# Half of the second output weight on the lower 64 partitions, loaded seven pairs earlier

## The chip, the cores and the metric

The kernel runs on one core of a Trainium2 chip. The metric is the device time of one execution in microseconds, as the median of several runs. Names used below: PE is the matrix engine (PEld its weight load), DVE the vector engine, ACT the scalar engine, POOL the general one, SP the engine that issues nearly all transfers. SBUF is the on-chip memory with 128 partitions, PSUM the accumulator memory of PE, HBM the main memory. Sixteen DMA engines carry the transfers of all queues.

## The reference: what is computed

Two attention blocks, A and B, each for one new token with a cache of 8192 keys and values, 32 heads of 128 elements. Both have one key and value head for each query head, so they are the same computation on different data:

```
q      = (x @ wq)                      # x: 1x512, wq: 512x4096, as 32 heads x 128
scores = q . k_cache * 128**-0.5       # k_cache: 32 x 8192 x 128
p      = softmax(scores)
o      = p @ v_cache                   # v_cache: 32 x 8192 x 128
out    = o (as 1x4096) @ wo            # wo: 4096 x 512
```

The result is the two 512-element rows side by side. All tensors are bf16. The caches are 64 MB each, four of them; wq and wo are 4 MB each. Each byte is used once, so nearly all the work is to move 285 MB from HBM into SBUF.

## The kernel before

The heads are taken in 32 pairs, 16 of A and 16 of B. In a pair, partitions 0 to 63 hold the first head and 64 to 127 the second, and each partition holds 128 consecutive tokens of its head (32 KB). K and V of a pair are one load of 4 MB each, into two buffers each (`kn`, `vn`, selected by the pair's parity).

For a pair `n`:

- `plan_mul` (L244): DVE multiplies K by the broadcast query in four pieces, in place.
- `plan_red` (L250): PE adds up over the 128 elements with the identity as the weight, in two halves of 16 matmuls; `plan_sr` (L263) and `plan_max` (L269) finish the scores and their maximum on DVE.
- `plan_gmax` (L275), `plan_exp` (L285): maximum over the partitions of a head, then the exponential on ACT, with the row sums; `plan_sum` (L304): PE adds the row sums over the partitions, DVE takes the reciprocal.
- `plan_pv` (L311): 128 small matmuls of V with the probabilities, in two halves; `plan_o` (L329) scales the result into two columns of `oD`, which holds for each of the 32 heads a column of 128 elements, one on each partition.

The work of pair n-1 after its exponential is interleaved with the start of pair n. The order on each engine is written out by hand: the main loop (L389 to L435) calls the planning functions, each appends to the engines' programs, and waits are put in where a result of another engine or a load is needed. SP issues every load of K, V and the weights on one queue, in the order of the calls; a K load into a buffer waits until the reduction of two pairs before has read it, a V load until the product of two pairs before has.

The output weight is loaded so that each of the 128 partitions gets consecutive rows (`load_wo`, L199). A group of `n` heads has 128n rows, so partition p holds rows p*n to p*n + n - 1 of the group. Since `oD` has its elements the other way round, `plan_relayout` (L350) turns the columns of a group: DVE spreads them over 128 columns with a mask, one matmul with a selector matrix sums them to the right partitions, and DVE copies the result into `o2`. `plan_wo` (L365) then multiplies: one matmul for each of the `n` rows that a partition holds, with a column of `o2` as the weight and 512 columns of wo, all adding up in one row of `qyp`; `plan_y` (L379) casts that row.

A's wo is one group of 32 heads. It goes into the space of the query weight (`wbuf`), is issued at pair 12, and its 32 matmuls follow in four pieces of eight after pairs 17 to 20. B's wo is split into groups of 16, 8, 4, 2 and 2 heads, so that the relayout of a group can follow as soon as its heads are done (after pairs 23, 27, 29, 30 and 31). All five loads are issued at pair 31, right behind V of pair 31, and all 32 matmuls stand at the end of PE's program, in the order of the groups.

`wo_sb` is a view of `wbuf` as 128 partitions of 32 rows of 512 elements. `jsel` and `mask` are the selector and the mask of a group size, made from the identity at the start (`plan_sel`, L338) for each size in `RG`.

Of the kernel before, what the change touches and what calls it, by code (L numbers as in the profile page):

```python
# [6 lines left out]
ALU = mybir.AluOpType  # L7
AX = mybir.AxisListType
BF16 = mybir.dt.bfloat16
F32 = mybir.dt.float32  # L10

P = 128
# [11 lines left out]
class _Plan:  # L24
# [15 lines left out]
    def op(self, eng, fn, ctr=None, needs=(), inc=1):  # L40

        for m in needs:
            self.wait(eng, m)
        if ctr is None:
            self.prog[eng].append(fn)
            return None
        ctr.n += inc
        self.prog[eng].append(lambda e: fn(e).then_inc(ctr.sem, inc))
        return ctr, ctr.n


def bass_concat_heads__mha_block_cached__gqa_block_cached__decode_kernel(
# [17 lines left out]
    wos = [A_wo, B_wo]  # L70
    NA = 2
    H, Sk, Dh = ks[0].shape[1:]
    D = xs[0].shape[2]
    NOUT = wos[0].shape[1]
# [7 lines left out]
    PA = H // 2  # L82
    NP = NA * PA
# [4 lines left out]
    DW = 512 // HT  # L88
    assert Dh % DW == 0

    WOG = [[(0, 32)], [(0, 16), (16, 8), (24, 4), (28, 2), (30, 2)]]
    RG = [32, 16, 8, 4, 2]

    with ExitStack() as st:
        ec = st.enter_context
# [2 lines left out]
        def sb(name, shape, dt):  # L98
            return ec(nc.sbuf_tensor(name, shape, dt))

        kn = sb("kn", [P, NK, T, Dh], BF16)
        vn = sb("vn", [P, NV, T, Dh], BF16)
        wbuf = sb("wbuf", [P, C * H * Dh], BF16)
        wq_sb = wbuf[:].rearrange("p (c n) -> p c n", c=C)
        wo_sb = wbuf[:].rearrange("p (j n) -> p j n", n=NOUT)
        qbc = sb("qbc", [P, NP, Dh], BF16)
        pt = sb("pt", [P, 2, T, 2], BF16)
        s_sb = sb("s_sb", [P, 2, T], F32)
# [11 lines left out]
        rinv = sb("rinv", [P, NP, 2], F32)  # L120
        oD = sb("oD", [P, NA, H], BF16)
        zb = sb("zb", [P, 2, P], BF16)
        o2 = sb("o2", [P, NA, H], BF16)
        mask = {g: sb("mask%d" % g, [P, P // g], BF16) for g in RG}
        jsel = {g: sb("jsel%d" % g, [P, g], BF16) for g in RG}
        out_sb = sb("out_sb", [1, NA, NOUT], BF16)

        def ps(name, shape):
            return ec(nc.psum_tensor(name, shape, F32))
# [5 lines left out]
        misc = ps("misc", [P, 512])  # L135
        qyp = ps("qyp", [P, 512])

        pl = _Plan()
        op, wait = pl.op, pl.wait

        def ctr(name):
            return _Ctr(nc, st, name)
# [3 lines left out]
        s_wo = [ctr("s_wo%d" % i) for i in range(5)]  # L146
# [4 lines left out]
        c_pool, c_dve, c_act, c_pe = ctr("c_pool"), ctr("c_dve"), ctr("c_act"), ctr("c_pe")  # L151
        c_mul, c_red, c_sr, c_pv = ctr("c_mul"), ctr("c_red"), ctr("c_sr"), ctr("c_pv")

        def dma(eng, dst, src, c, needs=()):
            return op(eng, lambda e: e.dma_start(dst, src), c, needs, inc=16)  # L155
# [21 lines left out]
        k_in, v_in, wq_in, wo_in = {}, {}, {}, {}  # L177
        red_done, pv_done, q_done, wo_done = {}, {}, {}, {}

        def load_k(n):  # L180
            a, i = divmod(n, PA)
            src = ks[a][0, 2 * i:2 * i + 2].rearrange("h (p t) d -> (h p) (t d)", p=HP)
            k_in[n] = dma("SP", kn[:, n % NK].rearrange("p t d -> p (t d)"), src, s_k[n % NK],
                          [red_done.get(n - NK)])

        def load_v(n, parts=1):
            a, i = divmod(n, PA)
            src = vs[a][0, 2 * i:2 * i + 2].rearrange("h (p t) d -> (h p) (t d)", p=HP)
            dst = vn[:, n % NV].rearrange("p t d -> p (t d)")
            w = T * Dh // parts  # L190
            v_in[n] = [dma("SP", dst[:, i * w:(i + 1) * w], src[:, i * w:(i + 1) * w],
                           s_v2 if i else s_v[n % NV], [pv_done.get(n - NV)])
                       for i in range(parts)]

        def load_wq(a):
            wq_in[a] = dma("SP", wbuf[:], wqs[a].rearrange("(p c) n -> p (c n)", p=P), s_w,
                           [q_done.get(a - 1)])

        def load_wo(a, g):  # L199
            h0, n = WOG[a][g]  # L200
            src = wos[a][h0 * Dh:(h0 + n) * Dh, :].rearrange("(p j) n -> p (j n)", p=P)
            wo_in[a, g] = dma("SP", wo_sb[:, h0:h0 + n, :].rearrange("p j n -> p (j n)"), src, s_wo[g],
                              [q_done[NA - 1] if a == 0 else wo_done[0]])


        for a in range(NA):
# [9 lines left out]
        misc_free, qy_free = [x_ready], [x_ready]  # L216
# [25 lines left out]
        mul_done, sr_done, p_done, m_done, r_done, o_done = {}, {}, {}, {}, {}, {}  # L242

        def plan_mul(n, c):  # L244
            k = kn[:, n % NK, c * CT:(c + 1) * CT, :]
            mul_done[n, c] = op("DVE", lambda e: e.tensor_tensor(  # L246
                k, k, qbc[:, n:n + 1, :].broadcast_to([P, CT, Dh]), ALU.mult),
                c_mul, [k_in[n], qbc_ready[n]])
# [87 lines left out]
        sel_ready = {}  # L336

        def plan_sel():  # L338
            for g in RG:
                v = ident[:].rearrange("p (s j) -> p s j", j=g)  # L340
                op("DVE", lambda e, g=g, v=v: e.tensor_reduce(mask[g][:], v, AX.X, ALU.max),
                   c_dve, [i_ident])
                sel_ready[g] = op("DVE", lambda e, g=g, v=v: e.tensor_reduce(
                    jsel[g][:], v.rearrange("p s j -> p j s"), AX.X, ALU.max), c_dve)

        z_n = [0]
        z_free = {}
        o2_ready = {}

        def plan_relayout(a, g):  # L350
            h0, n = WOG[a][g]
            z = z_n[0] % 2
            z_n[0] += 1
            s = P // n
            zv = zb[:, z, :].rearrange("p (h s) -> p h s", s=s)
            m = op("DVE", lambda e: e.tensor_tensor(
                zv, oD[:, a, h0:h0 + n].unsqueeze(2).broadcast_to([P, n, s]),
                mask[n][:, None, :].broadcast_to([P, n, s]), ALU.mult),
                c_dve, [sel_ready[n], o_done[a * PA + (h0 + n) // 2 - 1], z_free.get(z)])
            z_free[z] = op("PE", lambda e: e.matmul(misc[:, 0:n], zb[:, z, :], jsel[n][:],  # L360
                                                    start=True, stop=True), c_pe, [m, misc_free[0]])
            o2_ready[a, g] = misc_free[0] = op("DVE", lambda e: e.tensor_copy(
                o2[:, a, h0:h0 + n], misc[:, 0:n]), c_dve, [z_free[z]])

        def plan_wo(a, g, j0=0, j1=None):  # L365
            h0, n = WOG[a][g]
            j1 = n if j1 is None else j1

            def mm(e):
                r = None  # L370
                for j in range(h0 + j0, h0 + j1):
                    r = e.matmul(qyp[0:1, :], o2[:, a, j:j + 1], wo_sb[:, j, :],  # L372
                                 start=(j == 0), stop=(j == H - 1))
                return r
            wo_done[a] = op("PE", mm, c_pe, [o2_ready[a, g], wo_in[a, g]] + ([qy_free[0]] if h0 + j0 == 0 else []))

        y_done = {}

# [10 lines left out]
        for n in range(NP + 1):  # L389
            last = n == NP  # L390
            if n + 1 < NP:
                load_k(n + 1)
            if not last:
                load_v(n, 2 if n == NP - 1 else 1)
            if n == 0:
                load_wq(1)
            if n == 12:
                load_wo(0, 0)
            if n == NP - 1:
                for g in range(len(WOG[1])):  # L400
                    load_wo(1, g)
            if not last:
                plan_mul(n, 0)
                plan_mul(n, 1)
            if n > 0:
                plan_sum(n - 1)
            if not last:
                plan_red(n, 0)
                plan_mul(n, 2)
                plan_mul(n, 3)  # L410
                plan_sr(n, 0)
                plan_red(n, 1)
            if n > 0:
                plan_pv(n - 1, 0, HT)
            if not last:
                plan_sr(n, 1)
                plan_max(n)
                plan_gmax(n)
            if n > 0:
                plan_pv(n - 1, HT, T)  # L420
            if not last:
                plan_exp(n)
            if n > 0:
                plan_o(n - 1)
            if 3 <= n < 7:
                plan_q(1, n - 3)
            if n == PA:
                plan_relayout(0, 0)
            if PA < n <= PA + 4:
                plan_wo(0, 0, 8 * (n - PA - 1), 8 * (n - PA))  # L430
                if n == PA + 4:
                    plan_y(0)
            for g, (h0, k) in enumerate(WOG[1]):
                if n == PA + (h0 + k) // 2:
                    plan_relayout(1, g)  # L435
        for g in range(len(WOG[1])):
            plan_wo(1, g)
        plan_y(1)
        for a in range(NA):
# [37 lines left out]
```

## Time and profile before

| what | value |
|---|---|
| median of 3 runs | 682.3 us (681.56, 682.30, 682.37) |
| profiled execution, its time | 681.27 us |
| profiled execution, its span | 679.8 us |
| mean granted clock of PE | 0.754 |
| PE busy | 479.0 us (70%) |
| DVE busy | 360.6 us (53%) |
| ACT busy | 43.9 us (6%) |
| read from HBM | 285.21 MB, 420 GB/s over the span |
| multiply of K, a quarter (L246), mean | 2282 ns |
| wo matmul (L372), mean of 64 | 443 ns |
| K load of B, issue to landing, median | 25.3 us |
| V load of B, issue to landing, median | 31.8 us |
| wo of A (4 MB), issue to landing | 42.1 us |
| wo of B, 2 MB / 1 MB / 512 KB / 2 x 256 KB | 27.7 / 29.7 / 30.5 / 30.7 us |

How to read it: the profile is one execution. Times in the timeline and the chain count from the start of the span. The span leaves out some 1.5 us of the execution's own time. A row of a group gives the line of the code, the engine, the operation with its output and inputs, and the shapes; "idle before" names what the engine had been waiting for. The slices cut the span into 40 equal parts, and a digit is the busy share in tenths. The granted clock of PE is either 0.5 or 1.0 of full speed at any moment.

### The profile page before, as it was taken

Reading aid. Unit: us, or ns where it says so; the run is one execution under the profiler, and the core shown is the slowest. Engines: PE = TensorE matmul, PEld = TensorE weight load, DVE = VectorE, ACT = ScalarE, POOL = GpSimd, SP = SyncE. Lnnn points to the kernel's source line nnn. Section 1 sums busy time; section 2 is a strip of 40 time slices with the busy share of each in tenths; the row PEclk is TensorE's granted clock in tenths of the full one; section 3 lists DMA queues with packets and bytes.
Section 4 is the critical chain, followed back from the end, with each engine's and each line's share of the span. In section 5 each row is a group of like instructions: output and inputs, shape, how many; then the busy total and the mean of one; then the engine's idle time right before and its main releaser. Section 6 shows DMA issues by size and latency. Waiting matters only on the chain.

```text
span 679.8 us, 11835 instructions
## 1 busy us (share of the span) xinstructions
PE 479.0 (70%) x5518; PEld 273.0 (40%) x5518; DVE 360.6 (53%) x344; ACT 43.9 (6%) x171; POOL 2.1 (0%) x13
## 2 busy tenths in 40 slices
PE   2673787877678766745667898677668767667786
PEld 1233443434444433432344454334445424344453
DVE  1563556656455665605655555666555566665550
ACT  1100000111000000000000000000000000000000
POOL 1000000000000000000000000000000000000000
PEclk9976887667787766676677887777787866677887
DMA  9999999999999999999999999999999999999992
GB/s 372 436 431 431 433 431 430 431 431 428 431 431 431 431 431 431 428 431 432 430 426 429 429 431 429 429 430 431 431 431 430 428 432 431 430 431 430 425 418 117
DMA packets 10568, 285.97 MB, mean 421 GB/s; under 512 B 1172, under 2 KB 1176, under 8 KB 1560
## 3 DMA queue, kind: packets, MB, share of 16 engines
q1 hardware_dynamic: 10516, 285.22, 97.8%
q8 instruction: 43, 0.70, 0.4%
q14 instruction: 5, 0.04, 0.0%
q10 hardware_dynamic: 4, 0.00, 0.0%
HBM read 285.21 MB, written 0.00 MB: 420 GB/s over the span
## 4 chain that ended last, share of the span: by engine, by line
DMA 65%; PE 24%; DVE 7%; issue 4%; SPq 0%
DMA kn<-in_A_k_cache_dram 31%; DMA kn<-in_B_k_cache_dram 30%; PE rps L255 22%; DVE kn L246 7%; DMA wbuf<-in_B_wo_dram 4%; PE qyp L372 1%; PE acc L321 0%; SPq L155 0%; DVE out_sb L380 0%; PE mtp L276 0%
## 5 line engine op out<-in xcount | busy, mean ns | idle before, releaser
L255 PE MATMUL rps<-kn,ident 128*128 128x512 bf16 x1024 | 292.7, 457 | 148.7 <-DVE kn L246 148.7
L246 DVE TENSOR_TENSOR kn<-kn,qbc 128x4096 bf16<-128x4096 bf16 x128 | 286.7, 2282 | 92.1 <-DMA kn<-in_A_k_cache_dram 64.3
L255 PEld LDWEIGHTS rps<-kn,ident 128*128 128x128 bf16 x1024 | 113.9, 114 | 315.3 <-DVE kn L246 146.8
L321 PEld LDWEIGHTS acc<-pt,vn 128*128 128x128 bf16 x4096 | 110.4, 97 | 14.2 <-issue 6.9
L264 DVE TENSOR_REDUCE s_sb<-rps 128x64 f32<-128x512 f32 x64 | 44.3, 692 | 130.7 <-PE rps L255 130.7
L321 PE MATMUL acc<-pt,vn 128*128 128x2 bf16 x4096 | 112.7, 163 | 0.0
L293 ACT ACTIVATE negb<-bmp 128x1 f32<-128x1 f32 x32 | 5.5, 171 | 596.1 <-PE bmp L289 596.1
L305 PE MATMUL misc<-rsum,ones_f 128*128 128x2 f32 x64 | 18.3, 356 | 30.8 <-ACT pt L300 30.8
L305 PEld LDWEIGHTS misc<-rsum,ones_f 128*128 128x128 f32 x64 | 15.6, 302 | 38.0 <-ACT pt L300 36.3
L331 DVE TENSOR_TENSOR oD<-acc,rinv 128x2 bf16<-128x2 f32 x32 | 5.1, 159 | 47.5 <-PE acc L321 47.5
L300 ACT ACTIVATE pt<-s_sb,negb 64x128 bf16<-64x128 f32 x64 | 27.9, 435 | 1.8
L279 DVE TENSOR_REDUCE gm<-mtp 1x2 f32<-1x128 f32 x32 | 8.9, 279 | 27.8 <-PE mtp L276 27.8
L289 PE MATMUL bmp<-gm,hrow 1*128 1x1 f32 x128 | 22.4, 275 | 0.5 <-DVE gm L279 0.5
L289 PEld LDWEIGHTS bmp<-gm,hrow 1*128 1x128 f32 x128 | 19.7, 218 | 1.3 <-issue 0.7
L372 PE MATMUL qyp<-wbuf,o 128*1 128x512 bf16 x64 | 18.1, 443 | 2.1 <-DMA wbuf<-in_B_wo_dram 2.1
L228 PE MATMUL qyp<-wbuf,xb 128*64 128x512 bf16 x64 | 13.1, 550 | 6.6 <-DMA wbuf<-in_A_wq_dram 4.5
L276 PE MATMUL mtp<-ident_f,m 128*1 128x128 f32 x64 | 12.1, 271 | 1.1 <-DVE m L270 1.1
L300 ACT ACTIVATION_READ_ACCUMULATOR pt<-s_sb,negb 64x1 f32 x64 | 11.6, 182 | 0.0
L372 PEld LDWEIGHTS qyp<-wbuf,o 128*1 128x1 bf16 x64 | 5.5, 92 | 11.4 <-issue 3.8
L270 DVE TENSOR_REDUCE m<-s_sb 128x1 f32<-128x128 f32 x32 | 9.2, 286 | 1.1
L228 PEld LDWEIGHTS qyp<-wbuf,xb 128*64 128x64 bf16 x64 | 4.1, 140 | 12.4 <-issue 7.1
L380 DVE CAST out_sb<-qyp 1x512 bf16<-1x512 f32 x2 | 1.4, 679 | 12.8 <-PE qyp L372 12.8
(29 smaller groups left out, 27.3 us busy)
## 6 DMA issues: line engine op xcount, KB each, us to landing
kn<-in_A_k_cache_dram SPq DMA_DIRECT2D x16, 4096.0 KB, 25.6
vn<-in_A_v_cache_dram SPq DMA_DIRECT2D x16, 4096.0 KB, 32.5
kn<-in_B_k_cache_dram SPq DMA_DIRECT2D x16, 4096.0 KB, 25.3
vn<-in_B_v_cache_dram SPq DMA_DIRECT2D x15, 4096.0 KB, 31.8
wbuf<-in_A_wq_dram SPq DMA_DIRECT2D x1, 4096.0 KB, 12.4
wbuf<-in_B_wq_dram SPq DMA_DIRECT2D x1, 4096.0 KB, 30.4
wbuf<-in_A_wo_dram SPq DMA_DIRECT2D x1, 4096.0 KB, 42.1
vn<-in_B_v_cache_dram SPq DMA_DIRECT2D x2, 2048.0 KB, 21.1
```

The lines of the kernel that those rows point to most:

```text
L228: r = e.matmul(qyp[hh * HP:(hh + 1) * HP, :].rearrange("p (i d) -> p i d", d=Dh), xb[:, a, c, hh * HP:(hh + 1) * HP], w, start=(c == 0), s ...
L246: mul_done[n, c] = op("DVE", lambda e: e.tensor_tensor(k, k, qbc[:, n:n + 1, :].broadcast_to([P, CT, Dh]), ALU.mult), c_mul, [k_in[n], qbc ...
L255: r = e.matmul(rps[:, h, :].rearrange("p (t d) -> p t d", d=DW), ident[:], kn[:, n % NK, h * HT:(h + 1) * HT, i * DW:(i + 1) * DW], start= ...
L264: sr_done[n, h] = op("DVE", lambda e: e.tensor_reduce(s_sb[:, n % 2, h * HT:(h + 1) * HT], rps[:, h, :].rearrange("p (t d) -> p t d", d=DW ...
L270: m_done[n] = op("DVE", lambda e: e.tensor_reduce(m1[:, n:n + 1], s_sb[:, n % 2, :], AX.X, ALU.max), c_dve, [sr_done[n, 1]])
L276: m = op("PE", lambda e: e.matmul(mtp[0:1, 0:P], m1[:, n:n + 1], ident_f[:], start=True, stop=True), c_pe, [m_done[n], i_identf, gm_done.g ...
L279: gm_done[n] = op("DVE", lambda e: e.tensor_reduce(gm[:, n, :], mtp[0:1, 0:P].rearrange("o (h p) -> o h p", h=2), AX.X, ALU.max), c_dve, [m])
L289: r = e.matmul(bmp[:, 0:1], hrow[0:1, h, :], gm[0:1, n, h:h + 1], start=(h == 0), stop=(h == 1))
L300: p_done[n] = op("ACT", lambda e, h=h, q=q: e.activation(pt[q, n % 2, :, h], s_sb[q, n % 2, :], AF.Exp, bias=negb[q, n:n + 1], scale=scale ...
L305: m = op("PE", lambda e: e.matmul(misc[:, 0:2], ones_f[:], rsum[:, n, :], start=True, stop=True), c_pe, [p_done[n], misc_free[0]])
L321: r = e.matmul(acc[:, n % 2, 0:2], vn[:, n % NV, t, :], pt[:, n % 2, t, :], start=(t == 0), stop=(t == T - 1))
L372: r = e.matmul(qyp[0:1, :], o2[:, a, j:j + 1], wo_sb[:, j, :], start=(j == 0), stop=(j == H - 1))
```

## The change

B's groups stay 16, 8, 4, 2 and 2 heads, but a group now has a third number, the rows of wo that one partition holds. For B's first group it is 32 instead of 16, so the group's 2048 rows lie on 64 partitions, 0 to 63, with 32 KB each, where A's wo has been. It is loaded by eight transfers of eight partitions each: partitions b, b+4, ..., b+28, for b = 0 to 3 and 32 to 35. They are issued at pair 24, behind V of that pair and ahead of K of pair 26 (K of pair 25 is issued first). Its relayout still follows pair 23, with a weight of 64 columns; its 32 matmuls, which now read 64 partitions, are done in four pieces of eight after pairs 27 to 30, ahead of the sum of the row sums.

The other four groups (16 heads, 2 MB) are still issued behind V of pair 31 on all 128 partitions. They go into the first K buffer, which the reduction of pair 30 was the last to read. Their 16 matmuls stand at the end of PE's program. `o2` becomes one tile for each group, and the mask and the selector for a group size of 16 are no longer made.

```diff
-    WOG = [[(0, 32)], [(0, 16), (16, 8), (24, 4), (28, 2), (30, 2)]]
-    RG = [32, 16, 8, 4, 2]
+    WOG = [[(0, 32, 32)], [(0, 16, 32), (16, 8, 8), (24, 4, 4), (28, 2, 2), (30, 2, 2)]]
+    RG = [32, 8, 4, 2]
...
+        wo_kn = kn[:, 0].rearrange("p t d -> p (t d)").rearrange("p (j n) -> p j n", n=NOUT)
...
+        def wo_rows(a, g):
+            h0, n, r = WOG[a][g]
+            if a == 0 or g == 0:
+                return n * Dh // r, wo_sb, 0
+            return P, wo_kn, h0 - WOG[1][1][0]
+
         def load_wo(a, g):
-            h0, n = WOG[a][g]
-            src = wos[a][h0 * Dh:(h0 + n) * Dh, :].rearrange("(p j) n -> p (j n)", p=P)
-            wo_in[a, g] = dma("SP", wo_sb[:, h0:h0 + n, :].rearrange("p j n -> p (j n)"), src, s_wo[g],
-                              [q_done[NA - 1] if a == 0 else wo_done[0]])
+            h0, n, r = WOG[a][g]
+            np_, tile, j0 = wo_rows(a, g)
+            src = wos[a][h0 * Dh:(h0 + n) * Dh, :].rearrange("(p j) n -> p (j n)", p=np_)
+            dst = tile[0:np_, j0:j0 + r, :].rearrange("p j n -> p (j n)")
+            need = [q_done[NA - 1]] if a == 0 else [wo_done[0]] if g == 0 else [red_done[NP - 2]]
+            if np_ == P:
+                wo_in[a, g] = dma("SP", dst, src, s_wo[g], need)
+                return
+
+            for b in [c + i for c in range(0, np_, 32) for i in range(4)]:
+                wo_in[a, g] = dma("SP", dst[b:b + 29:4, :], src[b:b + 29:4, :], s_wo[g], need)
...
         def plan_relayout(a, g):
-            s = P // n
-            zv = zb[:, z, :].rearrange("p (h s) -> p h s", s=s)
+            w = P // r
+            m_ = n * w
+            zv = zb[:, z, 0:m_].rearrange("p (h s) -> p h s", s=w)
...
-        def plan_wo(a, g, j0=0, j1=None):
+        def plan_wo(a, g, i0=0, i1=None):
...
-                for j in range(h0 + j0, h0 + j1):
-                    r = e.matmul(qyp[0:1, :], o2[:, a, j:j + 1], wo_sb[:, j, :],
-                                 start=(j == 0), stop=(j == H - 1))
+                for i in range(i0, i1):
+                    res = e.matmul(qyp[0:1, :], o2[a, g][0:np_, i:i + 1], tile[0:np_, j0 + i, :],
+                                   start=(g == 0 and i == 0), stop=(end and i == r - 1))
...
-            if n == NP - 1:
-                for g in range(len(WOG[1])):
-                    load_wo(1, g)
+            if n == 24:
+                load_wo(1, 0)
...
+            if 27 <= n < 31:
+                plan_wo(1, 0, 8 * (n - 27), 8 * (n - 26))
+            if n == NP - 1:
+                for g in range(1, len(WOG[1])):
+                    load_wo(1, g)
-        for g in range(len(WOG[1])):
+        for g in range(1, len(WOG[1])):
             plan_wo(1, g)
```

More of the change, by code (lines that the diff above doesn't have):

```diff
@@ L122, in bass_concat_heads__mha_block_cached__gqa_block_cached__decode_kernel @@
         zb = sb("zb", [P, 2, P], BF16)
-        o2 = sb("o2", [P, NA, H], BF16)
+        o2 = {(a, g): sb("o2_%d_%d" % (a, g), [P, r], BF16)
+              for a in range(NA) for g, (_, _, r) in enumerate(WOG[a])}
         mask = {g: sb("mask%d" % g, [P, P // g], BF16) for g in RG}
@@ L350, in plan_relayout @@
         def plan_relayout(a, g):
-            h0, n = WOG[a][g]
+            h0, n, r = WOG[a][g]
             z = z_n[0] % 2
             z_n[0] += 1
-            s = P // n
-            zv = zb[:, z, :].rearrange("p (h s) -> p h s", s=s)
+            w = P // r
+            m_ = n * w
+            zv = zb[:, z, 0:m_].rearrange("p (h s) -> p h s", s=w)
             m = op("DVE", lambda e: e.tensor_tensor(
-                zv, oD[:, a, h0:h0 + n].unsqueeze(2).broadcast_to([P, n, s]),
-                mask[n][:, None, :].broadcast_to([P, n, s]), ALU.mult),
-                c_dve, [sel_ready[n], o_done[a * PA + (h0 + n) // 2 - 1], z_free.get(z)])
@@ L360, in plan_relayout @@
-            z_free[z] = op("PE", lambda e: e.matmul(misc[:, 0:n], zb[:, z, :], jsel[n][:],
+                zv, oD[:, a, h0:h0 + n].unsqueeze(2).broadcast_to([P, n, w]),
+                mask[r][:, None, :].broadcast_to([P, n, w]), ALU.mult),
+                c_dve, [sel_ready[r], o_done[a * PA + (h0 + n) // 2 - 1], z_free.get(z)])
+            z_free[z] = op("PE", lambda e: e.matmul(misc[0:m_, 0:r], zb[:, z, 0:m_], jsel[r][:],
                                                     start=True, stop=True), c_pe, [m, misc_free[0]])
@@ L362, in plan_relayout @@
             o2_ready[a, g] = misc_free[0] = op("DVE", lambda e: e.tensor_copy(
-                o2[:, a, h0:h0 + n], misc[:, 0:n]), c_dve, [z_free[z]])
-        def plan_wo(a, g, j0=0, j1=None):
-            h0, n = WOG[a][g]
-            j1 = n if j1 is None else j1
-            def mm(e):
-                r = None
-                for j in range(h0 + j0, h0 + j1):
-                    r = e.matmul(qyp[0:1, :], o2[:, a, j:j + 1], wo_sb[:, j, :],
-                                 start=(j == 0), stop=(j == H - 1))
-                return r
-            wo_done[a] = op("PE", mm, c_pe, [o2_ready[a, g], wo_in[a, g]] + ([qy_free[0]] if h0 + j0 == 0 else []))
+                o2[a, g][0:m_, :], misc[0:m_, 0:r]), c_dve, [z_free[z]])
@@ new lines, in plan_wo @@
+        def plan_wo(a, g, i0=0, i1=None):
+            h0, n, r = WOG[a][g]
+            i1 = r if i1 is None else i1
+            np_, tile, j0 = wo_rows(a, g)
+            end = g == len(WOG[a]) - 1
+            def mm(e):
+                res = None
+                for i in range(i0, i1):
+                    res = e.matmul(qyp[0:1, :], o2[a, g][0:np_, i:i + 1], tile[0:np_, j0 + i, :],
+                                   start=(g == 0 and i == 0), stop=(end and i == r - 1))
+                return res
+            wo_done[a] = op("PE", mm, c_pe, [o2_ready[a, g], wo_in[a, g]] + ([qy_free[0]] if g == i0 == 0 else []))
@@ L432, in bass_concat_heads__mha_block_cached__gqa_block_cached__decode_kernel @@
                     plan_y(0)
-            for g, (h0, k) in enumerate(WOG[1]):
+            for g, (h0, k, r) in enumerate(WOG[1]):
                 if n == PA + (h0 + k) // 2:
                     plan_relayout(1, g)
-        for g in range(len(WOG[1])):
+            if 27 <= n < 31:
[4 more added lines that the diff above has]
+        for g in range(1, len(WOG[1])):
             plan_wo(1, g)
```

## The prediction

> **What bounds the kernel now.** I read the page first (slices and queues), then the chain of waits, then the last 40 us: timeline, stretches, DMA.
>
> ```profile
> DMA  9999999999999999999999999999999999999992
> GB/s 372 436 431 431 433 431 430 431 431 428 431 431 431 431 431 431 428 431 432 430 426 429 429 431 429 429 430 431 431 431 430 428 432 431 430 431 430 425 418 117
> q1 hardware_dynamic: 10516, 285.22, 97.8%
> DMA 65%; PE 24%; DVE 7%; issue 4%; SPq 0%
> ```
>
> One queue moves 285 MB at 431 GB/s with no gap until the last slice. Every byte still has to be moved, so a gain can come only from the end, where the transfers stop and the last pair, the output product and the result follow. The chain of waits from 595 to 680 us (start, length, what):
>
> ```profile
> 640.89 27.70 DMA wbuf<-in_B_wo_dram
> 668.59 0.04 issue
> 668.63 8.68 PE qyp L372 x32
> 677.32 0.02 issue
> 677.34 0.68 DVE out_sb L380
> ```
>
> The first wo load of B (16 heads) lands at 668.6 and releases 32 matmuls in 8.68 us. From the last cast (ends 678.02) to the span's end is 1.78 us. Beside it stands the chain of pair 31, in the timeline:
>
> ```profile
> 642.69 4.49 DVE L246 TENSOR_TENSOR kn<-kn,qbc 128x4096 bf16<-128x4096 bf16 x2 [1.73 <-DMA kn<-in_B_k_cache_dram]
> 647.24 9.13 PE L255 MATMUL rps<-kn,ident 128*128 128x512 bf16 x32 [4.82 <-DVE kn L246]
> 662.23 3.55 PE L321 MATMUL acc<-pt,vn 128*128 128x2 bf16 x128
> 666.59 0.16 DVE L362 CAST o<-misc 128x2 bf16<-128x2 f32 x1 [0.28 <-PE misc L360]
> ```
>
> K31 has landed at 642.69, the DVE having waited 1.73 us for it; the last relayout is done at 666.75. So the tail of pair 31 takes 24.06 us, and PE then waits only 1.9 us for wo. Two chains lie 1.9 us apart: whatever comes ahead of K31 in the queue delays the second.
>
> How the transfers end, in stretches of 4 us and for the wo matmuls alone (length, busy PE and PEld (count), in the first fence DVE, ACT and POOL too, granted clock, DMA share, GB/s):
>
> ```profile
> 656.00:660.00 4.00, 4.00 (x133) 3.62 (x132) 1.26 (x4) 0.00 (x0) 0.00 (x0) 1.00 0.99 420
> 660.00:664.00 4.00, 2.88 (x74) 2.71 (x75) 0.77 (x4) 1.15 (x5) 0.00 (x0) 0.71 0.92 376
> 664.00:668.00 4.00, 1.97 (x68) 1.80 (x65) 0.61 (x3) 0.00 (x0) 0.00 (x0) 0.50 0.52 219
> 668.00:672.00 4.00, 3.37 (x9) 1.02 (x10) 0.00 (x0) 0.00 (x0) 0.00 (x0) 0.51 0.44 173
> 672.00:676.00 4.00, 4.00 (x20) 1.56 (x19) 0.00 (x0) 0.00 (x0) 0.00 (x0) 1.00 0.03 13
> ```
> ```profile
> 668.50:671.90 3.40, 3.27 (x8) 0.98 (x9) 0.50 0.43 170
> 671.90:675.30 3.40, 3.40 (x17) 1.34 (x16) 1.00 0.05 18
> ```
>
> From 664 to 672 the DMA share is one half: eight of the sixteen engines are done 8 us before the other eight. The trace's count of landings (16 semaphore increments a load) agrees: for K31, eight at 634.0 to 637.1 (six of them by 634.5, then 635.6 and 637.1), eight at 642.1 to 642.7; for the last wo load, 663.4 to 666.5 and 671.4 to 673.5. At the first load all sixteen lay within 0.7 us. The late half falls behind by some 1.6 us at a time, 43 times in all, and the instruction queue has 43 packets. I call the halves early and late. The last fence shows the clock: 8 wo matmuls in 3.4 us at 0.50, then 24 in 5.4 us at 1.00.
>
> **The change, part by part.**
>
> *Bytes.* 2 MB of wo move from behind V31 to behind V24, ahead of K26 to V31. The queue is never empty: a K load lands 25 us after its issue and takes 9.71 us, so some 15 us of transfers lie ahead of it. Total bytes stay.
>
> *Which engines carry them.* No row shows a load to eight partitions. Rows on either side: a 4 MB load to 128 partitions is 128 packets of 32,768 bytes, eight an engine; the one-partition x row is one packet on one engine. So eight partitions should be eight packets on eight engines, and eight such loads put 64 packets on the same eight, 8 x 1.21 = 9.7 us each, nothing on the rest. The lower end is an even spread, 4.85 us on each of sixteen. Which eight: the second x row's packet pushes back one stream of large packets, and that stream is one of the early half. It starts among the first, as do most of the early ones; the late ones mostly start later. I take the early half, and keep the others as rivals.
> The Trainium skill ("DMA: Bandwidth & Descriptors", section on why a DMA adds 16 to its semaphore) says that such a load runs on the largest number of engines up to 16 that divides the outermost dimension, the lowest-numbered ones; that would be eight, and the sum is the same if these are the early half. Its rules for kernel authors want 128 partitions outermost to use all sixteen, which speaks against this form of load; that rule supposes engines that finish together, and the stretch 664 to 668 (share 0.52) shows that they don't.
>
> *K31.* The early half reaches it 9.7 us later: 643.7 to 646.8, the laggard last; the late half still at 642.7. So K31 lands 4.15 us later, at 646.84, and pair 31 follows: 646.84 + 24.06 = 670.9 for the last relayout. In the other pairs the stretch from first multiply to end of exp is 18.3 to 20.2 us (18.99 here), so this is good to about 0.8 us. V31's second half lands at 656.6 + 9.7 = 666.3; its matmuls start at 668.2, covered by 1.9 us.
>
> *The remaining wo.* The late half ends 4.85 us sooner (668.6), the early half 4.85 later (laggard 671.4). The 1 MB group comes 2.4 us ahead of the last, at 669.0; PE needs it from 670.95. Landed in time: the wait on wo goes, and pair 31 is late next.
>
> *The last matmuls.* 16 instead of 32. Eight at 0.427 us and eight at 0.225: 5.2 us; all at the low clock: 6.8. Which, depends on where the clock's step falls (it went up at 671.90, 3.3 us after the start; another step is 3.4 us on). I take the middle, 6.0. The same for before: 8.7 to 10.3; the profiled run had the shortest.
>
> *Moved matmuls.* Four times 8, after pairs 27 to 30, in front of the sum of the row sums. The same eight for A took 3.08 us at 384.6; PE then idles 4.82 us before the next reduction (row at 647.24). 3.1 to 3.4 fit, and the reciprocal, queued behind two multiplies, doesn't wait for them. The first of them adds a wait on the wo load, issued three pairs (58 us) earlier against 42 us to landing for A's wo; behind it in PE's order stand the sum and the next reduction. Cost nothing; were the cover gone, 3.4 us once, in pair 31.
>
> *Eight issues instead of one.* 0.33 to 0.43 us each on SP, 3.4 us after V24's issue at 483.05; the next, K26, waits for a reduction that SP saw at 499.4 before. Hidden by 13 us. Eight loads in a row might leave gaps on the engines: the four last wo loads, 1 MB to 256 KB, land 2.4, 1.3, 0.7 and 0.6 us apart, within 0.1 us of their bytes; so 0 to 0.8 us, I take 0.
> The same page puts a fixed 2.0 us on each DMA (measured on another queue); taken as not overlapped, eight would add 16 us, against at most 0.1 us a load in those rows.
>
> *Relayout.* The 16-head relayout goes at pair 24, with half the columns; the two selector reductions for 16 go, ahead of K0's landing. Nothing either way.
>
> *Sum.* 670.95 + 6.0 = 676.95; cast and output 2.48 as before: span 679.4. The profiled run was 681.27 for a span of 679.8, so 1.47 outside: **681.0**. That run is the fast end of its kind: median 682.3 (681.56 to 682.37). The middle for before, 668.63 + 9.5 + 2.48 + 1.47 = 682.1, meets that median, so like is compared with like: 1.1 to 1.3 us less, close to 0.2%, about what a measurement here tells from no change.
>
> **Rivals.**
> 1. *Spread over sixteen.* K31 lands 4.85 later, 647.55; relayout 671.6; 677.65; 681.6. For: full loads use sixteen. Against: one packet a row.
> 2. *The late half, or a mixture with any late engine, carries them* (slower). K31 lands at 652.4, relayout 676.45, matmuls to 682.5: 686.4. For: no row names the engines; against: the x row's stream. It decides from the point where K31 slips by more than about 5.3 us, since the halved product saves 1.9 + 3.5.
> 3. *Clearly faster.* The moved matmuls keep the clock up, so that the last reduction takes its best (mul to exp 18.3, 0.7 less) and the 16 run warm, 3.6: 677.8. Or the laggard is not late in every run: K31 1.5 instead of 4.15 later gives 678.2. For: both rows vary. Against: pairs 18 to 20, with A's matmuls before them, took 18.8 to 19.3, and the laggard's slips come at regular distances.
> 4. *A gap in the queue, or an 8-load cost.* 0.8 us or more on the early half: 681.8 and up.
>
> **How the numbers follow.** Forecast (early half): 0.70, 679.8 to 682.3; rival 1: 0.06; rival 2: 0.13; rival 3: 0.07; rival 4: 0.04. The range leaves out rival 2 and part of 3 and takes in the rest: 678.6 to 683.4. Faster by over 0.2% (below 680.9): about 0.46 of the forecast, 0.2 of rival 1, rival 3: 0.40. Slower (above 683.7): rival 2, half of rival 4, and a little of the forecast: 0.18. The rest, 0.42, is within.
>
> **What would show it.** DMA share near 1 up to some 668 and then a short fall, not 8 us at one half; first multiply of pair 31 near 646.8; the last wo matmuls released by the relayout, 16 of them; none of the four chunks followed by a longer wait of the reduction. Wrong if K31 lands past 648, or if PE still waits for a wo load at the end.

## The result, and the profile after

The changed kernel takes 685.5 us (median of 4 runs, 684.89 to 686.29), the kernel before 681.93 us (4 runs, 680.97 to 682.37). The ratio is 1.0058, with a 95% interval of 1.0043 to 1.0072: 3.6 us slower, where 1.3 us less was forecast. The page after:

```profile
span 684.6 us, 11872 instructions
DMA  9999999999999999999999999999999999999990
q1 hardware_dynamic: 10500, 285.22, 97.2%
DMA 62%; PE 26%; DVE 8%; issue 4%; ACT 0%; SPq 0%; ACTq 0%
```

The bytes are the same, and the queue is as full as before. In the tail of the timeline of the changed kernel, the wait on wo is gone and the last relayout releases 16 matmuls, as forecast:

```profile
651.94 4.49 DVE L264 TENSOR_TENSOR kn<-kn,qbc 128x4096 bf16<-128x4096 bf16 x2 [1.72 <-DMA kn<-in_B_k_cache_dram]
656.49 9.37 PE L273 MATMUL rps<-kn,ident 128*128 128x512 bf16 x32 [3.38 <-DVE kn L264]
671.63 3.55 PE L339 MATMUL acc<-pt,vn 128*128 128x2 bf16 x128
675.88 6.45 PE L393 MATMUL qyp<-kn,o 128*1 128x512 bf16 x16
682.37 0.68 DVE L401 CAST out_sb<-qyp 1x512 bf16<-1x512 f32 x1 [6.22 <-PE qyp L393]
```

K31 lands at 651.94, not at 642.69: 9.25 us later. From there to the first of the last matmuls are 23.94 us, as before (24 us). So the loss is in one place, the landing of K31. The DMA share from 655 to 680 us, in 40 slices of 0.625 us, says why; before first, then after:

```profile
DMA  9999899999999665644454454421000000000000
```
```profile
DMA  9999899989999999996553211111121110000000
```

Before, half of the engines worked on alone for 8 us (digits 4 to 6). After, the share falls from 666 on and then stays at 1 until about 676: two of the sixteen engines carry on alone. The trace's landings (one semaphore step for each engine of a load) say the same. In V24, the load just ahead of the early ones, eight engines landed at 527.1 to 530.4 us and the eight late ones at 533.3 to 535.5, 6.2 to 8.3 us behind the foremost. A full load takes an engine 9.7 us. In K26, the first load behind the early ones, two engines land at 537.0 and 537.1 and six at 543.5 to 545.2, about a full load behind V24: two early ones and six late ones that carried nothing more. Six land at 546.6 to 549.8 and two at 552.8 and 553.3: six early ones and two late ones, each 9.6 us later than a full load alone would put them. Those two late engines land K26 some 16 us behind the foremost engine, and they set K26 to K31 and V31. The semaphore of the eight loads moved nine times for each load: one step at once, and one for each of eight engines. (Full loads move it sixteen times.) So the loads did run on eight engines, always the same eight, but these were not the early half.

### The profile page after: what moved, and what is told of

Read it like the earlier page. It is cut to its first block, busy times and chain, and to the rows that moved or that the text cites. A ratio compares the mean times of both kernels' runs of the same rounds, so it can differ in the third digit from the quotient of the medians.

```text
span 684.6 us, 11872 instructions
## 1 busy us (share of the span) xinstructions
PE 487.1 (71%) x5534; PEld 273.7 (40%) x5534; DVE 360.0 (53%) x342; ACT 43.9 (6%) x171; POOL 2.1 (0%) x13
## 4 chain that ended last, share of the span: by engine, by line
DMA 62%; PE 26%; DVE 8%; issue 4%; ACT 0%; SPq 0%; ACTq 0%
DMA kn<-in_B_k_cache_dram 31%; DMA kn<-in_A_k_cache_dram 31%; PE rps L273 23%; DVE kn L264 8%; PE acc L339 1%; PE qyp L393 1%; DVE out_sb L401 0%; PE bmp L307 0%; ACT pt L318 0%; PE mtp L294 0%; PE misc L323 0%; SPq L159 0%; DVE zb L375 0%; PE misc L379 0%; ACT negb L311 0%
## 5 line engine op out<-in xcount | busy, mean ns | idle before, releaser
L393 PE MATMUL qyp<-wbuf,o 128*1 128x512 bf16 (+1 forms) x64 | 22.4, 510 | 0.0
L393 PEld LDWEIGHTS qyp<-wbuf,o 128*1 128x1 bf16 (+1 forms) x64 | 5.6, 96 | 9.9 <-issue 6.2
L393 PE MATMUL qyp<-kn,o 128*1 128x512 bf16 x16 | 6.4, 590 | 0.0
```

Source lines behind the costliest of these rows:

```text
L393: res = e.matmul(qyp[0:1, :], o2[a, g][0:np_, i:i + 1], tile[0:np_, j0 + i, :], start=(g == 0 and i == 0), stop=(end and i == r - 1))
```

## The experiments

There were three theories at the start. Theory 1: the early loads run on eight fixed engines, six early and two late. Theory 2: any 2 MB ahead of K31 cost this. Theory 3: eight small loads leave gaps. Further ones, named by letters, are explained where they come up. Where the kernel before was run beside these, its median was 681.4 to 681.6 us.

| run | heads early, how | K31 lands | last matmuls | time, us | ratio to before (95%) |
|---|---|---|---|---|---|
| changed kernel | 16, eight loads of 8 partitions | 651.9 | 16 | 685.5 | 1.0058 (1.0043 to 1.0072) |
| e1_even16 | 16, one load of 128 | 647.7 | 16 | 681.45 | 1.0005 (0.9996 to 1.0014) |
| e2_noload | none | 642.8 | 16 | 677.5 | 0.994 (0.9924 to 0.9956) |
| e3_eight8 | 8, four loads of 8 | 647.1 | 24 | 682.54 | 1.0023 (1.0011 to 1.0035) |
| e4_six8 | 8, five loads of 6, one of 2 | 653.6 | 24 | 689.75 | 1.0124 (1.0107 to 1.0141) |
| e5_six6 | 6, four loads of 6 | 647.1 | 26 | 683.41 | 1.0028 (1.0016 to 1.004) |
| e6_contig8 | 16, eight loads of 8, neighbours | 671.0 | 16 | 705.39 | 1.0351 (1.0335 to 1.0366) |
| e7_halfpv | as before, half of the V matmuls | 640.8 | 32 | 678.82 | one run |
| e8_upper | 16, eight loads of 8, upper half | 668.9 | 16 | 704.61 | one run |
| e9_probe | as before, eight loads added | 645.8 | 32 | 684.74 | one run |
| e10_four4 | 4, four loads of 4 | 642.7 | 28 | 680.38 | 0.9983 (0.9973 to 0.9993) |

(K31: start of pair 31's first multiply in the profiled execution; in e1 it was not waiting for K31, which landed 0.03 us before.)

### Spread over all engines (e1_even16)

```diff
-    WOG = [..., [(0, 16, 32), (16, 8, 8), (24, 4, 4), (28, 2, 2), (30, 2, 2)]]
-    RG = [32, 8, 4, 2]
+    WOG = [..., [(0, 16, 16), (16, 8, 8), (24, 4, 4), (28, 2, 2), (30, 2, 2)]]
+    RG = [32, 16, 8, 4, 2]
...
-                plan_wo(1, 0, 8 * (n - 27), 8 * (n - 26))
+                plan_wo(1, 0, 4 * (n - 27), 4 * (n - 26))
```

> The same 16 heads at the same place (pair 24), but as one load to 128 partitions, 16 rows each, so spread over all sixteen engines; 16 early matmuls in four pieces of four. Theory 1 (the loads of eight partitions run on eight fixed engines, six of the early half and two of the late one, so that these two reach K31 9.7 us later): here every engine gets 4.85 us, K31 lands near 647.5 instead of 651.9, the last relayout is done near 671.6, 16 matmuls of 5.2 to 6.8 us end near 677.6, and the time is some 681.6, about that of the kernel before. Theory 2 (any 2 MB ahead of K31 cost this much, whichever engines carry them): K31 near 652 again, 685.5. Theory 3 (eight small loads leave gaps): as theory 1, 681.6.

Measured: 681.45 us, no different from before, the last relayout at 671.14. Theory 2 falls: the same bytes at the same place cost 4 us less when all engines carry them. It also prices the move itself: K31's delay of 5.0 us takes back all that the shorter product gives. Theory 3 would give the same time here; it falls by the rate of the changed kernel's queue, 426 to 433 GB/s in every stretch of 5 us from 525 to 565 us, which leaves no room for gaps.

### Without the early load (e2_noload)

```diff
             if n == 24:
-                load_wo(1, 0)
+                wo_in[1, 0] = None
```

> The changed kernel without the eight early loads; its 32 early matmuls read what lies there (wo of A), so the output of B lacks its first 16 heads of the product. It measures the half of the sum that has nothing to do with the early bytes. All theories: K31 lands at 642.7 as before, the last relayout is done near 666.8, the remaining 2 MB of wo land by 668.6, the 16 matmuls end near 672.8, and the time is some 676.8 (676 to 677.6). If it stays above 680, the halved product at the end is not worth what the prediction put on it.

This kernel leaves out the early half of B's wo, so it is no version to use. Measured: 677.5 us, 4 us below the kernel before. In its timeline:

```profile
642.82 4.49 DVE L264 TENSOR_TENSOR kn<-kn,qbc 128x4096 bf16<-128x4096 bf16 x2 [0.92 <-DMA kn<-in_B_k_cache_dram]
667.87 6.46 PE L393 MATMUL qyp<-kn,o 128*1 128x512 bf16 x16
```

K31 is where it was before, and the halved product ends 3 us sooner. The time lies inside what was expected (676 to 677.6); all of the loss belongs to the early bytes.

### Eight heads on eight engines, or on six (e3_eight8, e4_six8)

e3 has the groups `(0, 8, 32), (8, 8, 8), (16, 8, 8), (24, 4, 4), (28, 2, 2), (30, 2, 2)`; e4 has these too and other loads:

```diff
-            for b in [c + i for c in range(0, np_, 32) for i in range(4)]:
-                wo_in[a, g] = dma("SP", dst[b:b + 29:4, :], src[b:b + 29:4, :], s_wo[g], need)
+            rows = [slice(b, b + 21, 4) for b in range(4)] + [slice(24, 30), slice(30, 32)]
+            for q in rows:
+                wo_in[a, g] = dma("SP", dst[q, :], src[q, :], s_wo[g], need)
```

> Only 8 heads early, on partitions 0 to 31, by four loads of eight partitions; groups of 8, 8, 4, 2 and 2 heads remain for the end (24 matmuls). Theory 1: the two late engines get 4.85 us, K31 lands near 647.5, relayout 671.6, 24 matmuls of 7.0 to 8.7 us, time near 683.4. Were the eight engines the early half: K31 at 642.7, time near 678.6. Theory 2: half of the bytes, half of the slip, about as theory 1. Theory 3: four gaps instead of eight, as theory 1.

> As the run with 8 heads and loads of eight partitions, same bytes, same place, same 24 matmuls, but in five loads of six partitions and one of two. Theory 1: six partitions run on the first six engines, all of the early half; no late engine carries any of it, these are 5 to 6 large packets (6.1 to 7.3 us) on each of six. The early ones reach K31 by 641.7, their laggard by 643.2 to 644.4, so K31 slips by 0.5 to 1.7 us; relayout 667.3 to 668.5, time 679.1 to 680.3, below the kernel before and some 3 to 4 us below the run with loads of eight partitions. Theories 2 and 3 (bytes ahead of K31, or the number of loads: six here, four there): the same as there or slower, 683 or more.

e3 came as theory 1 has it (682.54; K31 at 647.07 for 647.5 expected): six early engines and two late ones are 4.9 us later at K26. e4 took 689.75 us, 7 us more than e3, where 3 to 4 less were expected. Its DMA rate over 495 to 560 us shows that something else went on (40 slices of 1.625 us):

```profile
GB/s 403 484 403 403 484 413 423 444 423 423 444 423 423 444 413 423 464 403 444 454 363 489 383 141 161 161 222 323 323 423 484 353 444 484 343 464 484 343 464 484
```

From 532 to 542 us the rate is 141 to 323 GB/s instead of 431, while the engines count as busy: all 34 packets of the full size that start from 532 to 538 us take 2.0 to 3.9 us instead of 1.21. (From 529 to 541 us, the stretch that the next expectation names, it is about half of them and not nearly all.) What sets two of the six loads apart is their rows, neighbouring ones among partitions 24 to 31 instead of every fourth one. That was my choice of rows, and made a new theory: that a queue is held up where an engine writes to partitions that another engine writes in the full loads (theory P), and not by loads of six as such (theory S).

### Are partitions what holds up the queue? (e5_six6, e6_contig8, e8_upper)

```diff
# e5_six6: groups (0, 6, 32), (6, 8, 8), (14, 8, 8), (22, 4, 4), (26, 4, 4), (30, 2, 2)
+            for b in range(4):
+                wo_in[a, g] = dma("SP", dst[b:b + 21:4, :], src[b:b + 21:4, :], s_wo[g], need)
...
# e6_contig8: the changed kernel, but
+            for b in range(0, np_, 8):
+                wo_in[a, g] = dma("SP", dst[b:b + 8, :], src[b:b + 8, :], s_wo[g], need)
...
# e8_upper: the changed kernel, but
+            dst = tile[P - np_:P, j0:j0 + r, :].rearrange("p j n -> p (j n)")
```

> 6 heads early on partitions 0 to 23, by four loads of six partitions b, b+4, ..., b+20; groups of 8, 8, 4, 4 and 2 heads at the end (26 matmuls). The run with six-partition loads and 8 heads was slow in a way no theory had: between 529 and 541 us nearly all packets of all sixteen engines took 2 to 3.9 us instead of 1.21. It had two loads in which the engines wrote to partitions (24 to 31) that other engines write in the full loads; the other four loads kept each engine to its own partitions. Theory P (engines that write to partitions of another engine hold up the whole queue): here nothing is held up; six early engines get four packets, 4.85 us, the laggard reaches K31 at 642.0, so K31 stays at 642.7; relayout 666.8, 26 matmuls of 7.5 to 9.1 us, time near 679.1 (678.2 to 680.2), below the kernel before. Theory S (loads of six, not a power of two, are what stalls the engines): packets of 2 to 4 us here too, K31 some 5 us later or more, time 685 or more.

> The changed kernel with one thing different: its eight loads go to partitions 0 to 7, 8 to 15, ..., 56 to 63 instead of every fourth partition. Same bytes, same number of loads and partitions. Theory P: in each load eight engines write to the partitions of two, packets are stretched several times, the queue's rate falls for some 20 us or more, K31 lands at least 10 us later than in the changed kernel (651.9), time 695 or more. Theory S: eight is a power of two, no stall, as the changed kernel: 685.5.

> The changed kernel with the eight loads sent to partitions 64 to 127 in the same steps; the 32 early matmuls still read partitions 0 to 63, which hold wo of A, so the output of B is not the reference's. Theory O (the engine follows from a packet's place in the load, so the same eight engines carry them and now write to partitions of the other eight): packets are stretched, K31 lands later than in the changed kernel (651.9), time above 687. Theory Q (the engine follows from the partition): the other eight carry them, two early ones and six late ones; no stretched packets, all late engines but two 9.7 us later, K31 near 652.4, time 685 to 686.5.

What theory P expects is what the runs show. e6, which differs from the changed kernel in the destination and source rows alone, takes 705.39 us, 20 us more. Stretches of 5 us of e6, then of the changed kernel (length, busy PE, PEld, DVE, ACT and POOL, granted clock, DMA share, GB/s):

```profile
530.00:535.00 5.00, 5.00 (x19) 2.02 (x18) 4.41 (x3) 0.00 (x0) 0.00 (x0) 0.79 1.00 198
540.00:545.00 5.00, 3.20 (x100) 2.76 (x101) 0.28 (x1) 0.00 (x0) 0.00 (x0) 0.74 0.94 223
```
```profile
530.00:535.00 5.00, 5.00 (x13) 1.79 (x12) 3.31 (x2) 0.00 (x0) 0.00 (x0) 0.51 1.01 433
540.00:545.00 5.00, 3.70 (x91) 3.35 (x89) 0.44 (x2) 1.15 (x5) 0.00 (x0) 0.67 1.00 429
```

The share stays near 1 at half the rate: busy time is not work. All of e6's packets of the full size that start from 530 to 545 us take 2.1 to 3.2 us. e8 has the source rows of the changed kernel and moves only the destination. It has 210 to 218 GB/s from 530 to 550 and packets of 2.4 to 2.55 us (the longest 2.76), twice the usual, and K31 lands at 668.9. That is what theory O expects (the engine follows from a packet's place in the load, so that the same eight engines now write to partitions of others); by theory Q (it follows from the partition) no packet would be stretched. Which engine writes which partition is in no row of the trace: that the steps of four partitions in the change keep each engine on its own is an inference from these three runs.

The Trainium skill ("DMA: Bandwidth & Descriptors", the part on back-pressure in remote DMA) says that a saturated destination port holds up the engines that share the path, for copies between cores. e6 and e8 look alike for loads from HBM, in that no packet of the stretches just named keeps its 1.21 us; whether the cause is the same no run here shows.

e5 has no stretched packets, so loads of six are not the trouble (theory S falls). But it missed its own number: 683.41 us instead of 679.1. Its timeline gives K31 at 647.08, 4.4 us late:

```profile
647.08 4.49 DVE L264 TENSOR_TENSOR kn<-kn,qbc 128x4096 bf16<-128x4096 bf16 x2 [2.10 <-DMA kn<-in_B_k_cache_dram]
671.04 8.73 PE L393 MATMUL qyp<-kn,o 128*1 128x512 bf16 x26
```

By its landings at K26, five early engines and one late one are 4.85 us later. So I had theory 1 wrong in one point: the first six engines are not the six early ones of the eight.

### Why a half is late (e7_halfpv)

```diff
-                for t in range(t0, t1):
+                for t in range(t0, t1, 2):
...
-                                 start=(t == 0), stop=(t == T - 1))
+                                 start=(t == 0), stop=(t == T - 2))
```

> The kernel before with every second matmul of V left out (64 instead of 128 a pair; its output is not the reference's). PE has some 4100 instructions fewer. Theory F (the late half is late because it also carries PE's instructions: 43 packets of 16 KB for 11036 instructions, 1.55 us of delay each): 27 packets in the instruction queue, and in K31's landings the late eight come some 5 us after the early six instead of 8.1 to 8.7. K31 near 639.5, first wo load of B near 665.3, time near 678.7. Theory G (late for another reason, such as the place of the engines): still 8 us behind, K31 at 642.7, first wo at 668.6, time within 1 us of the kernel before.

Measured: 678.82 us, K31 at 640.83. The queues:

```profile
q1 hardware_dynamic: 10516, 285.22, 98.1%
q8 instruction: 27, 0.44, 0.3%
```

There are 27 packets of instructions instead of 43, and in K31's landings seven of the late eight come 4.9 to 5.3 us after the foremost and one 6.8, instead of 8.1 to 8.7. That one made K31 later than the 639.5 expected. The time also has the shorter product of V in it, so the landings are the evidence, and this is one run.

The traces show the cause packet by packet. In the kernel before, the packets of q1 fall into sixteen streams, in which each packet starts as another ends. From 40 to 640 us these have 40 gaps of over 0.5 us, and there are 40 packets of instructions: each gap opens within 0.03 us of the start of one of them. A gap is 1.06 us long, and in 31 of the 40 cases the packet behind it takes some 1.7 us instead of 1.21; together that is 1.55 us. In e7 it is 25 gaps and 25 packets. So the late half is late because it also carries PE's instructions (theory F), and theory G, that it is late for another reason, falls.

### Which engines (e9_probe), and the version that follows (e10_four4)

```diff
# e9_probe, on the kernel before
...
+            if 21 <= n < 29:
+                k = n - 20
+                rows = wos[1][0:128 * 32, :].rearrange("(p j) n -> p (j n)", p=P)
+                b = (k - 1) % 4 + 32 * ((k - 1) // 4)
+                probe = dma("SP", wbuf[b:b + 4 * k - 3:4, :], rows[b:b + 4 * k - 3:4, :], s_pr, [wo_done[0]])
...
# e10_four4: groups (0, 4, 32), (4, 8, 8), (12, 8, 8), (20, 4, 4), (24, 4, 4), (28, 2, 2), (30, 2, 2)
...
+            for b in range(4):
+                wo_in[a, g] = dma("SP", dst[b:b + 13:4, :], src[b:b + 13:4, :], s_wo[g], need)
```

> The kernel before with eight loads more, whose data nobody uses: at pairs 21 to 28, behind V, one load of 1, 2, ... 8 partitions of 32 KB each (every fourth partition). If a load of k partitions always runs on the same first k engines (theory O), the landings of the following loads show, after the load of k partitions, exactly k engines 1.21 us later, always the same ones and one more each time. The one that is hit eight times carries the x row too and is an early one. From the earlier runs, of the first six engines exactly one must be late (loads of six delayed five early engines and one late one) and of the first eight two (loads of eight delayed six and two); this run says which. Theory R (a load takes k engines in turn): the delays fall on changing engines, 36 packets spread over all sixteen. Time: by theory O K31 slips by 1.21 us for each packet on the worst late engine, 1.2 to 8.5 us, so 682 to 690; by theory R some 2.7 us, 684 to 685.

> 4 heads early on partitions 0 to 15, by four loads of four partitions b, b+4, b+8, b+12, so on the first four engines, four packets (4.85 us) each; groups of 8, 8, 4, 4, 2 and 2 heads at the end (28 matmuls). The run with loads of six delayed one late engine, as its landings show, and so K31 by 4.4 us. If that late engine is not among the first four: K31 stays at 642.7 (laggard of the early ones 642.0), relayout 666.8, 28 matmuls of 8.0 to 9.6 us, time 679.5 (678.7 to 680.3), below the kernel before by 2 us or so. If it is among them: K31 near 647.1, time near 684.

In e9's landings, worked out from the trace's semaphore record, each load of k partitions puts exactly k streams 1.2 us further behind, the same ones each time and one more. In the order in which they join, their places behind the foremost just before are: five early ones (k = 1 to 5), then a late one at 7.9 us (k = 6), a late one at 8.0 (k = 7), and an early one at 0.1 (k = 8). So, counted in this order, engines 0 to 4 and 7 are early, 5 and 6 late, and theory R (each load takes its engines in turn) falls. It falls by the landings alone: the time, 684.74 us, fits both theories. The first stream, which by the prediction also carries the x rows, is an early one, as the prediction had it.

e10 uses the first four alone. It takes 680.38 us, which is faster than before by 0.17% (0.07 to 0.27%), and it is the one version here that does all the work and beats both kernels. K31 is on time:

```profile
642.73 4.49 DVE L264 TENSOR_TENSOR kn<-kn,qbc 128x4096 bf16<-128x4096 bf16 x2 [1.09 <-DMA kn<-in_B_k_cache_dram]
667.62 8.96 PE L393 MATMUL qyp<-kn,o 128*1 128x512 bf16 x28
```

It comes just past the slow edge of what was expected (678.7 to 680.3), 1.15 us below the kernel before where some 2 were expected: in the profiled execution the pair's tail took 24.9 us, 0.8 more than in the kernel before. A version with five partitions a load, or more than four packets an engine, was not tried.

## Why the prediction was wrong

- *What bounds the kernel, and two chains 1.9 us apart*: right. e1 shows the trade: 5.0 us of delay (4.85 in rival 1) for half of the product, and no change (681.6 expected of rival 1, 681.45 measured).
- *Which engines carry them*: the step that failed. Eight engines and one packet a row were right, and so were 9.7 us on each (9.6 measured). "I take the early half" was wrong: it rested on one engine of the eight, the x row's, and on the order of the first packets. Two of the eight (the sixth and seventh by e9) are late ones. Rival 2, "a mixture with any late engine", given 0.13, is what happened: 686.4 forecast, 685.5 measured.
- *K31*: 4.15 us later forecast, 9.25 measured; this follows from the step before it. By the threshold in rival 2 (slower from 5.3 us on) the sign follows too.
- *The remaining wo*: "landed in time, the wait on wo goes" was right, in another way: the two late engines land last, at about 676, but the relayout is as late.
- *The last matmuls*: 6.0 us forecast, 6.45 measured (e1 6.15, e2 6.46), inside 5.2 to 6.8. With the early bytes left out (e2) the gain is 4 us, less than the 1.9 + 3.5 that the prediction put on the halved product: in e2's profiled execution the pair's tail, from first multiply to the last matmuls, took 25.05 us and not 23.94.
- *Moved matmuls*: hidden. The reduction of pair 31 waited 3.38 us after them; the stretch from first multiply to the last matmuls is unchanged.
- *Eight issues*: mis-sized, but hidden. They took 5.77 us on SP, 0.72 each, not 0.33 to 0.43. They were over at 508.8, and the next issue came at 519.04. The prediction also read this stretch one pair too early: the issues at 483.05 and 499.4 are those of V23 and K25. V24's is at 503.0 and K26's at 519.36, just as far apart, so that nothing hangs on it.
- *Gaps between small loads* (rival 4): none: in the changed kernel the queue ran at 426 to 433 GB/s from 525 to 565 us.

The range ended at 683.4 and left rival 2 out. The evidence for "early" spoke of one engine; the prediction's own words on the order at the start ("as do most of the early ones", "mostly start later") could have warned that the groups are not clean.

## What to carry to other kernels

When transfers bound a kernel, look at how unevenly the engines end, and at what else they carry: here PE's instructions cost eight of them 8 us. A load of k partitions, for k from 1 to 8, ran on the same k engines each time in e9, so it can fill engines that end early, but only if all k of them do: identify them one by one (e9) before placing bytes, and stop at the first late one. Take partitions in steps of four, which kept the rate at 426 to 433 GB/s here, and not neighbours or the upper half, which halved the queue's rate (e6, e8). Count the delay of the next load on the critical path against what the moved bytes save.

## What was not expected

- The eight engines that carry PE's instructions are not the upper eight: by e9 the sixth and seventh of the first eight are among them. Each of their packets of 16 KB delays its engine by some 1.55 us, more than a data packet of twice the size (1.21 us).
- Eight-partition loads to neighbouring partitions, or to the upper half, halve the rate of the whole queue: 198 to 223 GB/s instead of 431 from 530 to 545 us in e6, 210 to 218 from 530 to 550 in e8. In e4, with a load of six neighbours and one of two, it is 141 at the lowest.
- A load to eight partitions in steps of four takes SP 0.72 us to issue, a load to 128 partitions 0.33 to 0.43. It is the steps and not the eight: e6's eight loads, which read and write neighbouring rows, took 2.73 us together, 0.34 each.
